# Order of the weight loads, a split first layer norm and a new priority table in an attention-plus-MLP kernel

## Chip, cores and metric

One core of a Trainium2 chip runs the whole kernel. The metric is device time in microseconds of one execution; the runs of a kernel are given by their median. The kernel before took 231.26 us (median of four: 230.19, 231.26, 231.27, 232.62).

## What is computed

One layer norm without weights feeds two branches, whose sum goes onto the input. Cut to what matters (S = 2048 rows, D = 512, 32 heads of 16, four segments of 512 rows, F = 1792; bf16):

```
xn = layernorm(x)                                   # (x - mean) / sqrt(var + 1e-5)
q, k, v = xn @ wq, xn @ wk, xn @ wv                 # split into 4 segments of 512 rows
for s in range(4):                                  # per head
    a_dot = softmax(q_s k_s^T / 4 + causal mask) v_s
    a_mem = phi(q_s) M / (phi(q_s) z + 1e-6)        # phi(t) = t + 1 where t > 0, else exp(t)
    o_s = g * a_mem + (1 - g) * a_dot               # g = sigmoid(beta), per head
    M += phi(k_s)^T v_s ;  z += sum(phi(k_s))
out = x + concat(o) @ wo + silu(xn @ w1) @ w2
```

## The kernel before

**Work and tiles.** Rows come in 16 tiles of 128, four per segment. TensorE makes, per segment, four tiles each of k, q (heads in eights) and v, fourteen tiles h of the MLP, the scores, the products with v (PV), the memory M, and the row products with w_2 and w_o. A gemm tile is four matmuls of 128x512 into one PSUM bank; a row product with w_2 is fourteen, with w_o four. Four banks (`ps`) serve all of these, and one buffer of four banks (`psS`) serves the scores.

**The beat.** Scores go in 72 quads, S0 to S71. Quad n needs `psS` free, so it waits for the exp of quad n-1 (E: 128x2048 on ScalarE, L890). GpSimd then masks the exp's result (M, L906, two instructions). Unit u is an eighth of the heads of a segment (16 units); PV u needs the masks of all quads with pieces of u, and two free banks. Between two scores TensorE has time for other matmuls, and the schedule fills it. VectorE empties the banks (kT, qT, V, hT "glu", EO, acc, o_t), ScalarE makes tanh for the MLP and the exp of phi, GpSimd the masked copies kB of k, the min of phi and small steps.

**Layer norm** (`ln`, L613). VectorE runs bn_stats and bn_aggr per tile (L621, L622; "stats"), GpSimd adds eps and raises to -0.5 (L629, L632; "rstd") for the groups of tiles in `LNG`, VectorE applies it (L640; "xn"). For segment 0, TensorE transposes xn and ScalarE (tiles 0 to 2) or VectorE (tile 3) copies it to xnT (L666, L668). For the other segments a DMA transpose from SP's queue does it (L674). phi(k) is transposed likewise into phiK (L781) for M.

**Memory and norm chains.** The softmax denominators go through DRAM and back in rows (L1101 to L1140, "Z": dZ, Zg, then a reciprocal on VectorE, a scaling Zr on GpSimd, dR, R), and so do the memory's (L1048 to L1077, "den"). VectorE then scales N with R (L1148, "a_t") and adds the memory's product psN (L1163, "oT").

**What sets the order.** Nothing is issued as it is written. Each step is a task with an engine, a guessed duration, dependences, the buffers that it takes, and a due time; `Sched.run` (L183) plays the tasks through and writes them out in the order that it finds: per engine the ready task with the least due time, scores and exps first. `Dn(n)` is a time, 12.5 + 2.3 n. `SHIFT` is a table by engine, label and count that shifts due times. The real waits (semaphores) are put in afterwards, from the buffers that instructions share; each DMA also waits for the landing of the eighth DMA before it. Each engine, and the DMA queue of SP, runs its list in that order without overtaking.

**Loads.** At the start (L456 to L478): x tiles 0 and 2 on SP's queue, 1 and 3 on ScalarE's; half of w_k on SP, half of w_q on ScalarE's, w_v on SP, the second half of w_q on ScalarE's, then on SP the first half of w_1 (896 KB), the second half of w_k, x tiles 4 to 7, the second half of w_1, beta. Later (`late_loads`, L1323): w_2 in two halves of 896 KB, w_o, and x of segments 2 and 3. There the planner may not start a load before a set time:

```
def at(k, n):
    k.ready = Dn(n)
    return k
for i, n in ((0, 6), (1, 9)):
    ld_2.append(at(load_w(w_2[:, c[i], :], kv(B_w2)[:, c[i], :], "SP", Dn(n), 5.5), n))
```

That time is the planner's alone. It settles the place in SP's order and makes no wait in the program.

Of the kernel before, what the change touches and what calls it, by code (L numbers as in the profile page):

```python
# [9 lines left out]
ALU = mybir.AluOpType  # L10
# [33 lines left out]
W2STEP = 2  # L44
NACC = 4
LOWB = 1
X3 = 37
LNG = ((0,), (1,), (2, 3))
XD = -1
SETUP = 9.0  # L50
HD = (12, 12)
LAST = 1
# [11 lines left out]
SEM = 0.05  # L64
SHIFT = {
    "DVE": {
        ("stats", 4): -4.9, ("stats", 5): -3.2, ("stats", 15): -0.9, ("xn", 13): -3.4,
        ("o_t", 12): 4.3,
    },
    "PE": {  # L70
        ("q1", 0): -9.5, ("q2", 0): -8.4, ("h0.0", 0): 21.4, ("h0.2", 0): 1.6, ("h0.4", 0): -10.5,
        ("h0.10", 0): 6.9, ("q4", 0): 7.2, ("k5", 0): -49.8, ("q5", 0): -4.6, ("k6", 0): 2.2,
        ("k7", 0): 15.9, ("q7", 0): 0.3, ("v10", 0): 14.1, ("v11", 0): -1.8, ("v12", 0): 18.7,
        ("v13", 0): -8.1, ("M0", 0): -9.3, ("w2.1", 0): -4.6, ("w2.3", 0): -1.8,
        ("wo.2", 0): 19.9, ("PV4", 0): 7.9, ("PV7", 0): 11.3, ("h1.0", 0): -69.3,
        ("h1.4", 0): -11.9, ("h1.6", 0): 41.7, ("h1.7", 0): 16.8, ("h1.10", 0): 13.8,
        ("h1.11", 0): -3.8, ("h1.12", 0): 16.4, ("h1.13", 0): -5.8, ("q8", 0): -2.2,
        ("k10", 0): -21.9, ("v22", 0): -9, ("M1", 0): 4.1, ("psN", 0): -21.9, ("w2.7", 0): 3.1,
        ("wo.4", 0): 13.2, ("wo.6", 0): 58.8, ("wo.7", 0): -7.6, ("PV8", 0): 9.2,
        ("PV10", 0): 8.6, ("h2.2", 0): 6.4, ("h2.3", 0): 11.6, ("h2.4", 0): 30.7,  # L80
        ("h2.5", 0): 7.1, ("h2.7", 0): -15.7, ("h2.8", 0): 5.8, ("h2.9", 0): -10.7,
        ("k13", 0): -12.4, ("v33", 0): 39.2, ("w2.8", 0): 4.3, ("w2.9", 0): -2.5,
        ("w2.10", 0): -50.3, ("w2.11", 0): 5.8, ("wo.9", 0): 5, ("wo.11", 0): 6,
        ("h3.3", 0): -14.2, ("h3.4", 0): -7.4, ("h3.8", 0): -15, ("h3.11", 0): -1.2,
        ("den3", 0): 52.5, ("outT3", 0): -2.2,
    },
    "ACT": {
        ("tanh", 6): -5.5, ("tanh", 18): -5.2,
    },
    "SP": {  # L90
        ("Z", 2): 30.5, ("Z", 10): 23.5, ("Z", 13): 18.6, ("Z", 23): -18.2, ("Z", 29): -3.1,
        ("den", 6): -3, ("den", 11): -9.4, ("den", 20): -36.7, ("mg", 4): 37.5,
    },
    "POOL": {
        ("phi", 13): -20.5, ("pq", 2): 3.8, ("kB", 22): 3.7, ("Zr", 2): 29, ("M58", 0): 50.8,
    },
}

# [222 lines left out]
def kernel(  # L321
# [25 lines left out]
    def sb(shape, dt, name):  # L347
        return cp.tile(shape, dt, name=name)
# [46 lines left out]
    rstd = sb([P, NT, 1], F32, "rstd")  # L395
    stt_t = [sb([P, nc.vector.BN_STATS_DIM], F32, f"st{i}") for i in range(4)]
    st_r = Ring(stt_t)
    lnc = sb([P, 2, 2], F32, "lnc")
    ident = sb([P, P], BF16, "ident")
    pm = sb([P, 2], F32, "pm")  # L400
# [46 lines left out]
    def load_w(dst, src, eng, due, vis, after=()):  # L447
        def fn():
            e = nc.sync if eng == "SP" else nc.scalar
            e.dma_start(out=dst, in_=src)  # L450
        return A(eng, 0.5, fn, due=due, vis=vis, seqdeps=after, label="w")
# [1 line left out]
    def kv(w):  # L453
        return w.rearrange("(ko ki) n -> ki ko n", ki=P)

    load_x(0, 1, "SP", 0, 2.85)  # L456
    load_x(1, 1, "ACTQ", 0, 2.95)
    load_x(2, 1, "SP", 0, 2.9)
    load_x(3, 1, "ACTQ", 0, 3.1)
    def halves(dst, src, n, which):  # L460
        c = slice(0, n) if which == 0 else slice(n, None)
        return dst[:, :, c], kv(src)[:, :, c]

    C2, F2 = D // 2, F // 2
    ld_o, ld_2 = [], []
    ld_k = [load_w(*halves(w_k, A_wk, C2, 0), "SP", 0, 5.2)]
    ld_q = [load_w(*halves(w_q, A_wq, C2, 0), "ACTQ", 0, 5.4)]
    ld_v = load_w(w_v[:], kv(A_wv), "SP", 0, 7.5)
    ld_q.append(load_w(*halves(w_q, A_wq, C2, 1), "ACTQ", 0, 7.0))
    ld_1 = [load_w(*halves(w_1, B_w1, F2, 0), "SP", 0.1, 9.5)]  # L470
    ld_k.append(load_w(*halves(w_k, A_wk, C2, 1), "SP", 0.15, 10.5))
    load_x(4, 2, "SP", 0.2, 11.5)
    load_x(6, 2, "SP", 0.2, 12.0)
    ld_1.append(load_w(*halves(w_1, B_w1, F2, 1), "SP", 0.3, 13.5))
    ld_b = load_w(
        bet[:], bass.AP(tensor=A_beta.tensor, offset=A_beta.offset, ap=[[0, P], [1, H]]),
        "SP", 0.35, 13.5,
# [1 line left out]
    def pool(dur, fn, deps=(), due=0.0, **k):  # L479
        return A("POOL", dur, fn, deps, due, **k)  # L480
# [130 lines left out]
                  mode="full", label="warm")  # L611

    def ln(s, due):  # L613
        for js in LNG if s == 0 else ((0, 1), (2, 3)):
            ag = []
            for j in js:
                t = s * TPS + j
                b = Buf(st_r)

                def f_st(t=t, b=b):  # L620
                    nc.vector.bn_stats(out=b.tile[:], in_=xt(t))  # L621
                    nc.vector.bn_aggr(out=mv[:, t, :], in_=b.tile[:])  # L622

                ag.append(A("DVE", 0.8, f_st, [xl[t]], due + 0.1 * j, takes=(b,), frees=(b,),
                            label="stats"))

            def f_r(t=s * TPS + js[0], n=len(js)):
                rs = rstd[:, t : t + n, :]
                nc.gpsimd.tensor_tensor(  # L629
                    out=rs, in0=mv[:, t : t + n, 1:2], in1=lnc[:, 0:n, 0:1], op=ALU.add  # L630
                )
                nc.gpsimd.tensor_tensor(out=rs, in0=rs, in1=lnc[:, 0:n, 1:2], op=ALU.pow)  # L632

            r = pool(1.0, f_r, ag + [c_ln], due + 0.1 * js[0], label="rstd")
            for j in js:
                t = s * TPS + j
                xb = Buf(xn_r)

                def f_x(t=t, xb=xb):
                    nc.vector.tensor_scalar(  # L640
                        out=xb.tile[:], in0=xt(t), scalar1=mv[:, t, 0:1],
                        scalar2=rstd[:, t, 0:1], op0=ALU.subtract, op1=ALU.mult,
                    )

                n = A("DVE", 0.35 if s == 0 else 0.48, f_x, [r], due + (XD if s == 0 else 0.1 * j),
                      takes=(xb,), frees=(xb,), label="xn")
                if s == 0:
                    pb = Buf(banks)

                    def f_t(xb=xb, pb=pb):  # L650
                        pv_ = pb.tile[:].bitcast(BF16)
                        for dt in range(DT):
                            nc.tensor.transpose(
                                pv_[:, dt * P : (dt + 1) * P], xb.tile[:, dt * P : (dt + 1) * P],
                                ident[:],
                            )

                    tr = A("PE", 0.26, f_t, [n, c_id], due, takes=(pb,), frees=(pb, xb), mode="full",
                           label="tr")
                    eng = "DVE" if j == 3 else "ACT"  # L660

                    def f_e(j=j, pb=pb, eng=eng):
                        o = xnT_b[0].tile[:, :, j * P : (j + 1) * P]
                        i = pb.tile[:].bitcast(BF16)[:, 0:D].rearrange("p (a b) -> p a b", a=DT)
                        if eng == "ACT":
                            nc.scalar.copy(out=o, in_=i)  # L666
                        else:
                            nc.vector.tensor_copy(out=o, in_=i)  # L668

                    e = A(eng, 0.5 if eng == "ACT" else 0.35, f_e, [tr], due,  # L670
                          takes=(xnT_b[0],), frees=(pb, xnT_b[0]), label="xnT")
                else:
                    def f_d(s=s, j=j, xb=xb):
                        nc.sync.dma_start(  # L674
                            out=xnT_b[s].tile[:, :, j * P : (j + 1) * P], in_=xb.tile[:],
                            transpose=True,
                        )
                    e = A("SP", 1.25, f_d, [n], due, vis=3.6, takes=(xnT_b[s],),
                          frees=(xb, xnT_b[s]), label="xnT")
                xnT_done[s].append(e)  # L680
# [186 lines left out]
    def quad(u, q):  # L867
# [21 lines left out]
        def f_x():  # L889
# [2 lines left out]
        e = A("ACT", 1.755, f_x, [sct], dn, vis=1.876 + 0.08, takes=(pb,), frees=(sbuf, pb),  # L892
              kind="exp", label=f"E{n}")
        last_exp[0] = e

        def f_m():
            for r in range(2):
# [343 lines left out]
    def tail():  # L1241
# [64 lines left out]
        for j in range(TPS):  # L1306
# [13 lines left out]
                nc.sync.dma_start(out=out_flat[t * P : (t + 1) * P, :], in_=ob.tile[:])  # L1320
            A("SP", 0.35, f_d, [e], 0, vis=1.75, frees=(ob,), label="out")

    def late_loads():  # L1323
        def at(k, n):
            k.ready = Dn(n)
            return k

        c = slice(0, FT // 2), slice(FT // 2, FT)
        for i, n in ((0, 6), (1, 9)):
            ld_2.append(at(load_w(w_2[:, c[i], :], kv(B_w2)[:, c[i], :], "SP", Dn(n), 5.5), n))  # L1330
        ld_o.append(at(load_w(w_o[:], kv(A_wo), "SP", Dn(12), 4.5), 12))
        load_x(8, 4, "SP", Dn(14), 4.5)
        load_x(12, 4, "SP", Dn(X3), 8.0, [xl[8]])
        at(xl[8], 14)
        at(xl[12], X3)

    ln(0, -4)
    for s in range(NSEG):
# [76 lines left out]
```

## Time and profile before

| | |
|---|---|
| median of four runs | 231.26 us |
| the profiled execution | 231.27 us |
| its span, first to last instruction | 229.5 us |
| TensorE clock granted | 0.998 |
| TensorE busy | 218.1 us (95%) |
| ScalarE, VectorE, GpSimd busy | 178.6, 173.4, 164.9 us |
| first score, last output step | 11.98 us, 225.75 us |
| DMA | 21.11 MB, mean 92 GB/s |

Times are microseconds from the first instruction. PE is TensorE's matmuls, PEld its weight loads, DVE VectorE, ACT ScalarE, POOL GpSimd, SP the engine that issues most DMAs; "SPq" marks an issue. L571 is the helper that records every matmul, so matmuls are told apart by their tiles. A line of waits reads: engine and line, what it waited for, total, times, longest. A line of the chain of waits: start, duration, what ran or was waited for. A line of the timeline: start, duration, engine, line, operation, tiles, count. Matmul ends are modelled: a 128x512 matmul is shown with 380 ns, though the next one starts 216 ns after it.

### The profile page before, as it was taken

What the parts mean: (1) busy time and instruction counts of PE and PEld (TensorE: products, weight loads), DVE (VectorE), ACT (ScalarE), POOL (GpSimd) and SP (SyncE); (2) the same over time, 40 slices, a digit from 0 to 9 for tenths busy, and PEclk for the clock granted to TensorE, in tenths of its full rate; (3) what the DMA queues carried; (4) which work ended last, traced back from release to release, by engine and by line L of the source; (5) the groups of instructions that cost most, each with busy time, mean ns of one, the idle gap of its engine ahead of it and who ended that gap; (6) DMA issues with size and microseconds to landing.
All of it is one profiled execution on the core that took longest, in us unless ns stands there. A gap on an engine that the chain in (4) does not pass through costs nothing.

```text
span 229.5 us, 6765 instructions
## 1 busy us (share of the span) xinstructions
PE 218.1 (95%) x2792; PEld 101.9 (44%) x2792; DVE 173.4 (76%) x302; ACT 178.6 (78%) x161; POOL 164.9 (72%) x285
## 2 busy tenths in 40 slices
PE   7799968999999999999999998999999999999993
PEld 7644433445444444434543444444454444445441
DVE  3689976698974789988894867988664798475972
ACT  2388995999898899896998796988898889895000
POOL 5749993897949659999999869689698465446500
PEclk9999999999999999999999999999999999999999
DMA  6975397341235221043256531010442200114202
GB/s 174 351 256 120 68 178 196 111 118 26 46 74 131 49 71 49 0 146 119 69 122 84 101 59 54 0 60 17 134 114 54 94 4 24 49 37 121 92 14 93
DMA packets 30708, 21.11 MB, mean 92 GB/s; under 512 B 15956, under 2 KB 29780, under 8 KB 30676
## 3 DMA queue, kind: packets, MB, share of 16 engines
q1 hardware_dynamic: 29332, 19.88, 33.7%
q10 hardware_dynamic: 1344, 0.79, 1.1%
q8 instruction: 22, 0.36, 0.7%
q14 instruction: 10, 0.08, 0.1%
HBM read 11.73 MB, written 2.64 MB: 63 GB/s over the span
## 4 chain that ended last, share of the span: by engine, by line
PE 71%; DMA 9%; DVE 9%; POOL 7%; issue 1%; SPq 1%; ACT 0%; POOLq 0%
PE ps L571 60%; PE psS L571 11%; POOL Pt L906 4%; DMA w_v<-in_A_wv_dram 4%; DMA xnT<-xn 3%; POOL kB L767 2%; DMA R<-dR 1%; DVE hT L1182 1%; DMA dR<-Zr 1%; DVE xn L640 1%; DVE V L827 1%; DVE st L621 1%; DVE kT L762 1%; DVE qT L810 1%; POOL pq L698 1%
## 5 line engine op out<-in xcount | busy, mean ns | idle before, releaser
L890 ACT ACTIVATE Pt<-psS 128x2048 bf16<-128x2048 f32 x72 | 135.6, 1883 | 20.3 <-PE psS L571 17.0
L906 POOL TENSOR_SCALAR_AFFINE_SELECT Pt<-Pt 64x512 bf16<-64x512 bf16 (+1 forms) x144 | 92.2, 641 | 34.9 <-ACT Pt L890 28.9
L571 PE MATMUL ps<-xnT,w 128*128 128x512 bf16 x224 | 57.4, 380 | 3.1 <-DMA xnT<-xn 3.1
L571 PE MATMUL ps<-w,hT 128*128 128x512 bf16 x196 | 48.7, 380 | 0.0
L1182 DVE SCALAR_TENSOR_TENSOR hT<-hT,ps 128x512 bf16<-128x512 bf16 x56 | 37.0, 678 | 10.2 <-ACT hT L1178 10.1
L1178 ACT ACTIVATE hT<-ps 128x512 bf16<-128x512 f32 x56 | 32.3, 605 | 2.8 <-PE ps L571 2.7
L571 PEld LDWEIGHTS <-w 128*128 128x128 bf16 x224 | 20.1, 98 | 26.8 <-issue 5.8
L571 PEld LDWEIGHTS <-hT 128*128 128x128 bf16 x224 | 20.3, 98 | 24.9 <-issue 2.6
L571 PE MATMUL psS<-qT,kB 32*128 32x256 bf16 (+5 forms) x640 | 28.7, 262 | 0.0
L767 POOL TENSOR_SCALAR kB<-kT,pm 128x512 bf16<-128x512 bf16 x30 | 22.6, 762 | 5.9 <-DVE kT L762 4.6
L571 PEld LDWEIGHTS <-kB 32*128 32x128 bf16 x640 | 11.6, 92 | 27.3 <-issue 25.9
L571 PE MATMUL ps<-Pt,VS 64*32 64x256 bf16 (+5 forms) x640 | 18.7, 261 | 1.6 <-DVE hT L1182 1.0
L571 PE MATMUL ps<-Pt,V 64*32 64x64 bf16 (+5 forms) x640 | 20.1, 260 | 0.0
L571 PE MATMUL ps<-xnT,w_q 128*128 128x512 bf16 (+1 forms) x76 | 18.3, 346 | 0.3 <-DMA w_q<-in_A_wq_dram 0.3
L571 PE MATMUL ps<-w_v,xnT 128*128 128x512 bf16 x64 | 17.7, 380 | 0.7 <-DMA w_v<-in_A_wv_dram 0.7
L571 PE MATMUL ps<-xnT,w_k 128*128 128x512 bf16 (+1 forms) x76 | 17.7, 346 | 0.0
L571 PEld LDWEIGHTS <-V 64*32 64x32 bf16 x640 | 14.0, 91 | 7.6 <-DVE hT L1182 2.5
L1207 DVE SCALAR_TENSOR_TENSOR acc<-ps,x_all 128x512 f32<-128x512 f32 x12 | 8.2, 681 | 8.9 <-PE ps L571 8.9
L962 DVE CAST N<-ps 128x512 bf16<-128x512 f32 x15 | 10.2, 682 | 5.7 <-PE ps L571 5.5
L571 PE MATMUL ps<-w_o,N 128*128 128x512 bf16 x54 | 14.3, 380 | 0.2 <-DVE V L827 0.2
L1084 POOL TENSOR_TENSOR pq<-pq,Dr 128x512 bf16<-128x512 bf16 x12 | 13.7, 1156 | 1.0 <-DMA Dr<-dE 0.6
L571 PEld LDWEIGHTS <-VS 64*32 64x32 bf16 x640 | 12.7, 91 | 2.4 <-DVE hT L1182 1.3
(96 smaller groups left out, 255.0 us busy)
## 6 DMA issues: line engine op xcount, KB each, us to landing
w<-in_B_w_dram SPq DMA_DIRECT2D x4, 896.0 KB
VS<-V SPq DMA_DIRECT2D x8, 264.0 KB
out_dram<-o_t SPq DMA_DIRECT2D x16, 128.0 KB
R<-dR SPq DMA_DIRECT2D x15, 128.0 KB
Dr<-dE SPq DMA_DIRECT2D x12, 128.0 KB
x_all<-in_A_x_dram SPq DMA_DIRECT2D x2, 512.0 KB
N<-O SPq DMA_DIRECT2D x12, 64.0 KB
w_k<-in_A_wk_dram SPq DMA_DIRECT2D x2, 256.0 KB
```

The costliest lines, as they stand in the source:

```text
L571: nc.tensor.matmul(o, lhsT=l, rhs=r, start=start, stop=stop, **k)
L621: nc.vector.bn_stats(out=b.tile[:], in_=xt(t))
L640: nc.vector.tensor_scalar(out=xb.tile[:], in0=xt(t), scalar1=mv[:, t, 0:1], scalar2=rstd[:, t, 0:1], op0=ALU.subtract, op1=ALU.mult,)
L698: nc.gpsimd.tensor_scalar(out=dst_b.tile[:], in0=dst_b.tile[:], scalar1=1.0, scalar2=0.0, op0=ALU.min, op1=ALU.max,)
L767: nc.gpsimd.tensor_scalar(out=kB[u].tile[:, :, KB * r : KB * r + KB], in0=kT[u].tile[:].rearrange("p (a b) -> p a b", b=KB), scalar1=pm[:, ...
L890: nc.scalar.activation(out=pb.tile[:], in_=psS[:], func=AF.Exp, scale=SCALE)
L906: nc.gpsimd.affine_select(out=v, in_=v, compare_op=ALU.is_ge, fill=0.0, base=0, pattern=pat, channel_multiplier=-1,)
L962: nc.vector.tensor_copy(out=dst.tile[:, dt, :], in_=buf.tile[:])
L1084: nc.gpsimd.tensor_tensor(out=pb.tile[:], in0=pb.tile[:], in1=rb.tile[:], op=ALU.mult)
L1178: nc.scalar.activation(out=hb.tile[:], in_=b.tile[:], func=AF.Tanh, scale=0.5)
L1182: nc.vector.scalar_tensor_tensor(out=hb.tile[:], in0=hb.tile[:], scalar=1.0, in1=b.tile[:], op0=ALU.add, op1=ALU.mult)
L1207: nc.vector.scalar_tensor_tensor(out=ab.tile[:], in0=b.tile[:], scalar=0.5, in1=xt(t), op0=ALU.mult, op1=ALU.add,)
```

## The change

Three things.

1. *Late loads.* The set times go. Instead `hold` gives a load's task a dependence on another task: w_2's first half on the four xnT transposes of segment 1, its second half on the exp of quad 9 (E9), w_o on E11, x of segment 2 on E13, x of segment 3 on E31. These are dependences among the planner's tasks.
2. *The start.* The second halves of w_q and w_k move behind the second half of w_1, all on SP; x tiles 4 to 7 move ahead of it. In segment 0 each row tile has its own rstd; eps is added on VectorE, behind bn_aggr, and GpSimd only raises to -0.5. Tile 2's mean and variance come from two ScalarE passes (Copy and Square, each with an accumulated sum), and two small VectorE operations bring them to the form that the rest expects. Tile 3's statistics may start no earlier than 6.4 us by the planner.
3. *The table.* `SHIFT` is another one, for VectorE, TensorE, GpSimd, ScalarE and SP, so the order changes on every engine, from the first layer norm to the last segment.

```diff
-X3 = 37
-LNG = ((0,), (1,), (2, 3))
+HOLD = {9: 1, 11: 2, 13: 3, 31: 4}
+LNG = ((0,), (1,), (2,), (3,))
+STJ = 3
+STR = 6.4
+ACTJ = 2
...
-    load_x(0, 1, "SP", 0, 2.85)
+    load_x(0, 1, "SP", 0, 3.4)
...
     ld_v = load_w(w_v[:], kv(A_wv), "SP", 0, 7.5)
-    ld_q.append(load_w(*halves(w_q, A_wq, C2, 1), "ACTQ", 0, 7.0))
     ld_1 = [load_w(*halves(w_1, B_w1, F2, 0), "SP", 0.1, 9.5)]
-    ld_k.append(load_w(*halves(w_k, A_wk, C2, 1), "SP", 0.15, 10.5))
-    load_x(4, 2, "SP", 0.2, 11.5)
-    load_x(6, 2, "SP", 0.2, 12.0)
-    ld_1.append(load_w(*halves(w_1, B_w1, F2, 1), "SP", 0.3, 13.5))
+    load_x(4, 2, "SP", 0.2, 9.8)
+    load_x(6, 2, "SP", 0.2, 10.0)
+    ld_1.append(load_w(*halves(w_1, B_w1, F2, 1), "SP", 0.3, 12.0))
+    ld_k.append(load_w(*halves(w_k, A_wk, C2, 1), "SP", 0.3, 12.5))
+    ld_q.append(load_w(*halves(w_q, A_wq, C2, 1), "SP", 0.3, 12.5))
...
+                if first and j == ACTJ:
+                    rt = float(D) ** -0.5
...
+                        nc.scalar.activation(
+                            out=scr[:], in_=xt(t), func=AF.Copy, scale=-rt / D, accum_out=nbias[:],
+                        )
...
+                        nc.scalar.activation(
+                            out=scr[:], in_=xt(t), func=AF.Square, scale=rt, bias=nbias[:],
+                            accum_out=vj,
+                        )
...
+                        nc.vector.tensor_scalar(
+                            out=vj, in0=vj, scalar1=EPS, scalar2=None, op0=ALU.add
+                        )
+                        nc.vector.tensor_scalar(
+                            out=mv[:, t, 0:1], in0=nbias[:], scalar1=-1.0 / rt, scalar2=None,
+                            op0=ALU.mult,
+                        )
...
+        if n in HOLD:
+            hold(late[HOLD[n]], [e])
...
+    def hold(t, deps):
+        for d in deps:
+            d.outs.append((t, True))
+            t.nwait += 1
...
+        for i in range(2):
+            ld_2.append(load_w(w_2[:, c[i], :], kv(B_w2)[:, c[i], :], "SP", Dn(6 + 3 * i), 6.5))
+        ld_o.append(load_w(w_o[:], kv(A_wo), "SP", Dn(12), 5.5))
         load_x(8, 4, "SP", Dn(14), 4.5)
-        load_x(12, 4, "SP", Dn(X3), 8.0, [xl[8]])
+        load_x(12, 4, "SP", Dn(37), 5.5)
+        late.extend([ld_2[0], ld_2[1], ld_o[0], xl[8], xl[12]])
+        hold(late[0], xnT_done[1])
```

## The prediction

> **What bounds the kernel.** I read the busy table first, then TensorE's waits, then the chain that ended last, then the stretch around the longest wait.
>
> ```profile
> PE 218.1 (95%) x2792; PEld 101.9 (44%) x2792; DVE 173.4 (76%) x302; ACT 178.6 (78%) x161; POOL 164.9 (72%) x285
> ```
>
> TensorE is the bound, but busy time alone can't say how tightly. The chain of waits can: from one score burst (psS) to the next it reads like this nearly everywhere:
>
> ```profile
> 61.21 0.33 PE psS L571 x12
> 61.54 2.26 PE ps L571 x10
> ```
>
> Ten 128x512 matmuls start 0.216 us apart, and the score with its two changes of tile shape costs 0.43, so a score period is 10 x 0.216 + 0.43 = 2.59 us. I took the start of all 72 scores from the trace and held each period against its own content. Priced so, the work from the first score (11.98 us) to the last matmul is 206.5 us; it took 213.9. A new order saves no TensorE work, only this difference. TensorE's waits:
>
> ```profile
> PE ps L571 <- DMA xnT<-xn: 3.1, 1, 3.1
> PE ps L571 <- DVE hT L1182: 1.0, 1, 1.0
> PE ps L571 <- DMA w_v<-in_A_wv_dram: 0.7, 1, 0.7
> PE ps L571 <- DVE N L1163: 0.7, 1, 0.7
> ```
>
> Against the period sum the same places cost more: the eighth period takes 6.29 us where 12 matmuls and a score need 3.02 (3.27 lost), the 33rd 3.99 for 2.66 (1.33), the 47th 3.57 for 2.45 (1.12). The other 1.7 us are scattered. The chain names what lay behind each:
>
> ```profile
> 2.19 8.09 DMA w_v<-in_A_wv_dram
> ...
> 28.72 6.68 DMA xnT<-xn
> ...
> 101.36 0.62 POOL pq L698
> 102.01 1.11 DVE pq L704
> 103.12 0.61 DVE hT L1182
> ...
> 131.78 3.02 DMA dR<-Zr
> 134.86 0.66 SPq L1140
> 135.57 3.36 DMA R<-dR
> 138.95 0.73 DVE N L1148
> ```
>
> See four different causes: a first weight that lands late; a transpose of 6.68 us; VectorE standing in order behind a GpSimd step; VectorE standing behind a round trip through DRAM. The transpose is the odd one. The DMA queue's own timeline:
>
> ```profile
> 20.27 2.61 SPq L674 DMA_TRANSPOSE xnT<-xn  x2
> 25.51 1.19 SPq L781 DMA_TRANSPOSE phiK<-pkT  x1
> 26.75 0.58 SPq L450 DMA_DIRECT2D w<-in_B_w_dram  x1
> 27.43 2.60 SPq L674 DMA_TRANSPOSE xnT<-xn  x2
> 30.36 5.61 SPq L781 DMA_TRANSPOSE phiK<-pkT  x2
> ```
>
> By the semaphores in the trace the transposes issued at 20.27 and 21.68 landed at 22.79 and 24.09, and the one at 25.51 at 27.80: 2.3 to 2.5 us each. Those at 27.43 and 28.72, behind the 896 KB load of w_2, landed at 34.92 and 35.40; w_2 itself at 34.26. Without it the last would have landed near 28.72 + 2.45 = 31.2, before TensorE wanted it (32.3).
>
> **The change, part by part.** *The holds.* They add dependences to the planner's tasks. The program built from them carries no wait for an exp on SP: each load there waits only for the DMA eight before it. What is real is the order on SP. Now all four xnT transposes and the second phiK go ahead of w_2's first half; third phiK, second half, fourth phiK, w_o and x8 follow. To price it, place the fourth xn on VectorE. It is busy without a gap from 13.16 to 28.46 in the trace, 24 operations up to and with that xn; now they are 26, with one more glu (0.65) and the four gcol operations (0.32), and it starts some 0.4 earlier: end at 28.46 - 0.4 + 0.97 = 29.0. Two transposes back to back (1.25 to issue, 2.45 to land) put the last xnT at 31.5 to 32. TensorE first wants it (q4) after the ninth score: 69 matmuls and one PV up to the eighth score where before there were 67, then nine: the eighth score at 30.64 - 0.63 (see the start) + 0.43, q4 at 30.44 + 0.43 + 9 x 0.216 + 0.43 = 33.2. Margin 1.3 us. Of what is queued behind on SP, the third phiK now lands behind w_2 (up to 7.5 us by the row above, near 40); its pkT buffer is next written after the 13th exp, near 46. The fourth phiK, behind w_2's second half, lands near 44, and M0 wants it near 47. **Gain 3.27**, bounds 0 (they collide anyway) and 3.27.
>
> [...]
>
> *The start.* The second half of w_q leaves the early queue (256 KB) and goes to the end, with k's. At the 313 to 391 GB/s that the windows from 5 to 15 us show that is 0.7 us less ahead of w_v, whose last part landed at 10.28; I take 9.6. Row statistics: the x tile's bn_stats and bn_aggr take 0.80 pitch on VectorE; tile 2's leave it for two passes on ScalarE, priced by the 128x512 copy there (0.59), so 1.2, in the idle time between the table load's end (4.12, now about 0.6 earlier, a w_q issue less ahead) and the first xnT copy (6.82). Bounds 0.9 and 3.8 (two exps of 128x2048). The added eps and var operations cost about 0.1 each (gcol: 0.32 for four), five of them. GpSimd's add (0.19, with its gap 0.27) falls out of every rstd. Sum: first xn at 5.40 instead of 5.79, last xn ends 8.45 instead of 8.93. But ahead of the fourth xnT copy VectorE now has a kB, which waits for ScalarE's kB, and a qT: copy ends near 10.35 (before 9.91). Then q0's last piece 10.4, its cast 10.8 to 11.2, first score 11.35 against 11.98; 0.63 earlier, less one matmul (0.22) that moved behind it. **Gain 0.4**, bounds -0.8 (if ScalarE's passes hold the copies 1.2) and 0.9.
>
> [...]
>
> *The table.* Same matmuls, one more behind the first score: 206.7 us. So it acts by cover alone. I counted for each PV how long after the last mask it needs TensorE comes to it. Before, eight of sixteen had under 0.5 us, PV6 among them, where TensorE lost 1.33; now six have: PV6 has 1.8 and PV5 2.0, and PV1, 8, 10, 12, 14 and 15 have 0.3 to 0.5, in stretches where GpSimd's masks run 0.07 to 0.9 late by the old rows. The first psN moves from the 46th to the 49th score. Its chain (GpSimd's Zr, then 7.2 us by the rows above to R) starts about one period later, so R lands 1.4 us before VectorE's a_t stands ready, but psN comes within 0.2 us of a_t. Both losses (2.45) may go; something else will be late. I book about half, as no row shows the new neighbours: **gain 1.25**, bounds -0.6 and 3.0.
>
> Sum on the profiled execution's span: 229.5 - 3.27 - 0.4 - 1.25 = 224.6. That run took 231.27, 1.77 more than its span and the median of the runs to 0.01: **226.3 us**.
>
> **The rivals.**
> *The other stalls keep their size, elsewhere.* For it: the planner guesses durations, and its first table left 4 us of late work behind. Then 229.5 - 3.27 - 0.4 + 1.77 = 227.6.
> *The holds do nothing.* No wait stands in the program; should phiK's wait for VectorE end early, or xn come late, w_2 meets the transposes again: 226.3 + 3.27 = 229.6. Against it: the phiK issued at 25.51, just ahead of w_2, was not disturbed.
> *GpSimd becomes the bound, and it is slower.* Between masks 25 and 36 GpSimd has 30.1 us of work (kB 0.69, phi 0.61, masks 0.9 and 1.37, pq 1.13, two rstd, Mbf, Zr) for 29.0 us of TensorE; before 28.6 for 28.7, and there masks already ran 1.83 us late. If every kB, phi and mask took its slowest row (1.23, 0.92, 1.71): 8 x 0.54 + 8 x 0.31 + 9 x 0.34 = 9.9 more, lag 11, less PV7's slack of 1.9: 9.1 lost. Against the 4.8 of transposes, start and 47th period: 235.6. It decides from a lag of 6.7. Against it: most rows sit at the median.
>
> **How the numbers follow.** Forecast 0.60 (224.2 to 227.5 alone), stalls elsewhere 0.21, holds idle 0.13, GpSimd 0.06. Low end 224.2: transposes, start 0.9 and all 3.0 of the later losses gone. High end 229.6: holds idle. Outside lie GpSimd and small tails. A measurement of this kernel tells about 1% from no change: faster means under 228.95. That holds the forecast and nearly all of the second case: 0.78; within 1%: 0.16; slower: 0.06.
>
> **What would show it.** Right: no TensorE wait for xnT; xnT landing 2.3 to 2.5 us after issue; the third phiK slow instead; w_v landing before 9.8; first score before 11.6; periods 33 and 47 without their loss. Wrong: a wait for xnT near 33; ScalarE's statistics ending after 6; masks over 2 us late near the 35th score; a new wait on VectorE of a microsecond or more, most likely before PV8, PV10 or psN.

## The result, and the profile after

The kernel after takes 232.93 us (median of 53 runs, 229.59 to 239.05); the kernel before 231.58 (79 runs, 229.89 to 234.38), and the forecast was 226.3, 6.6 us less. The ratio of the two kernels is 1.0014, 95% interval 0.9995 to 1.0032: by it, no difference that can be measured. It is taken over the fast runs alone, those within 1.5% of a kernel's fastest, which leaves out 23 of the 53 runs after; the medians of all runs stand 0.6% apart, and the section on the clock comes back to this. The profiled execution after took 231.89 us, span 230.1 (before 229.5), granted clock 0.998.

Busy table and TensorE's waits of the kernel after:

```profile
PE 218.7 (95%) x2792; PEld 102.1 (44%) x2792; DVE 171.8 (75%) x305; ACT 180.0 (78%) x165; POOL 164.4 (71%) x283
```

```profile
PE ps L577 <- DVE O L1009: 2.4, 2, 1.8
PE ps L577 <- DVE hT L1229: 1.7, 1, 1.7
PE psS L577 <- POOL ident masks.py:199: 1.4, 1, 1.4
PE ps L577 <- DVE qT L846: 0.8, 1, 0.8
PE ps L577 <- POOL Pt L953: 0.7, 1, 0.7
PE ps L577 <- DVE pq L749: 0.4, 1, 0.4
```

The busy table says nothing, as before. In the waits, the 3.1 us for xnT and the 0.7 for w_v are gone, and two VectorE lines stand in their place. (The line with `ident` is the wait ahead of the first matmuls, 1.4 us; both kernels have it.) SP's timeline after shows why xnT is no longer late:

```profile
21.98 9.57 SPq L719 DMA_TRANSPOSE xnT<-xn  x4
31.65 1.22 SPq L826 DMA_TRANSPOSE phiK<-pkT  x1
32.92 0.58 SPq L456 DMA_DIRECT2D w<-in_B_w_dram  x1
33.60 1.20 SPq L826 DMA_TRANSPOSE phiK<-pkT  x1
```

The four transposes, issued at 21.98, 23.28, 28.84 and 30.34, land 2.4 to 2.5 us later, the last at 32.84. The phiK transpose issued at 33.60, just behind w_2's half, is the slow one now: it lands at 40.10.

Priced as in the prediction (0.216 us per matmul, 0.43 per score), the 71 score periods lost 7.12 us before and 8.18 after:

| period (n-th score after the first) | lost before, us | lost after, us |
|---|---|---|
| 8 | 3.27 | 0.26 |
| 27 | below 0.1 | 0.61 |
| 31 | below 0.1 | 1.83 |
| 33 / 34 | 1.33 / below 0.1 | below 0.1 / 0.45 |
| 44 | below 0.1 | 2.00 |
| 47 | 1.12 | 0.36 |
| 65 and 67 | below 0.1 each | 0.89 and 0.80 |

So 3.01 us were won at the eighth period, and 4.1 lost elsewhere, net. The last score starts 1.15 us later (207.41 for 206.26): first score 0.34 earlier, losses 1.06 more, and two matmuls (0.43) that moved between the two; behind the last score some 0.5 is saved. Where the new losses begin stands in VectorE's timeline:

```profile
81.83 0.69 DVE L1009 CAST O<-ps 128x512 bf16<-128x512 f32 x1 [1.41 <-DMA N<-O]
...
83.64 0.94 DVE L1168 RECIPROCAL Zf<-Zg 128x128 f32<-128x128 bf16 x1
...
91.83 1.52 DVE L1195 TENSOR_TENSOR N<-N,R 128x512 bf16<-128x512 bf16 x2
93.52 0.62 DVE L1195 TENSOR_TENSOR N<-N,R 128x512 bf16<-128x512 bf16 x1 [0.17 <-DMA R<-dR]
94.06 1.64 DVE L749 SCALAR_TENSOR_TENSOR pkT<-kT,pkT 128x512 bf16<-128x512 bf16 x1
95.63 0.08 DVE L749 DVE_READ_ACCUMULATOR pkT<-kT,pkT 128x1 f32 x1
95.63 0.68 DVE L1229 SCALAR_TENSOR_TENSOR hT<-hT,ps 128x512 bf16<-128x512 bf16 x1
...
131.87 0.69 DVE L1009 CAST O<-ps 128x512 bf16<-128x512 f32 x1 [2.78 <-DMA N<-O]
```

The bracket is idle time and what ended it. There is one buffer O. It is free for the next unit only when four small DMAs have copied its rows into N (N<-O, "mg"). VectorE stands 1.41 and 2.78 us for them (periods 27 and 44). Period 31 is VectorE's order: three products with R and a pkT step stand ahead of the hT at 95.63 that TensorE waits for. The third product starts as its R lands (93.49; idle 0.17 us), the first two take 0.73 and 0.86 us where most others take 0.41 to 0.43, and the pkT step takes 1.64 where others take 0.66 to 1.15; what stretches these is not shown. SP's queue shows why N<-O is late (here `x4` and `x2` count issues, and the time is that of issuing them):

```profile
76.12 1.21 SPq L826 DMA_TRANSPOSE phiK<-pkT  x1
77.42 2.52 SPq L1163 DMA_DIRECT2D N<-O  x4
...
123.52 3.14 SPq L826 DMA_TRANSPOSE phiK<-pkT  x2
126.75 2.49 SPq L1163 DMA_DIRECT2D N<-O  x4
```

The new table puts phiK transposes, and in the first segment the den chain (dD, Dg), ahead of them. They land at 81.71 and 131.65. Before, they were issued from 70.92, landed at 76.07, and O was wanted at 81.80.

### The profile page after: what moved, and what is told of

The parts are those of the page before. It is cut to its first block, busy times and chain, and to the rows that moved or that the text cites. A ratio compares the mean times of both kernels' runs of the same rounds, so it can differ in the third digit from the quotient of the medians.

```text
span 230.1 us, 6774 instructions
## 1 busy us (share of the span) xinstructions
PE 218.7 (95%) x2792; PEld 102.1 (44%) x2792; DVE 171.8 (75%) x305; ACT 180.0 (78%) x165; POOL 164.4 (71%) x283
## 4 chain that ended last, share of the span: by engine, by line
PE 67%; DVE 9%; DMA 8%; POOL 7%; SPq 3%; issue 3%; ACT 2%; DVEq 0%; POOLq 0%; ACTq 0%
PE ps L577 54%; PE psS L577 13%; POOL Pt L953 3%; DMA N<-O 2%; POOL pq L1131 2%; SPq L1163 2%; DMA R<-dR 2%; DMA Dr<-dE 2%; DVE kT L807 1%; DVE hT L1229 1%; DVE pkT L749 1%; DMA dR<-Zr 1%; DVE N L1009 1%; SPq L826 1%; DVE O L1009 1%
## 5 line engine op out<-in xcount | busy, mean ns | idle before, releaser
L577 PE MATMUL ps<-w,hT 128*128 128x512 bf16 x196 | 47.5, 380 | 0.0
L812 POOL TENSOR_SCALAR kB<-kT,pm 128x512 bf16<-128x512 bf16 x30 | 20.6, 696 | 6.4 <-DVE kT L807 5.1
L577 PE MATMUL ps<-Pt,V 64*32 64x256 bf16 (+5 forms) x640 | 19.8, 260 | 0.7 <-POOL Pt L953 0.7
L577 PE MATMUL ps<-w_v,xnT 128*128 128x512 bf16 x64 | 16.6, 380 | 1.1 <-DVE qT L846 0.8
L577 PE MATMUL ps<-xnT,w_q 128*128 128x512 bf16 (+1 forms) x76 | 17.5, 346 | 0.0
L1009 DVE CAST O<-ps 128x512 bf16<-128x512 f32 x15 | 10.2, 682 | 4.2 <-DMA N<-O 4.2
```

What stands on the lines that cost most here:

```text
L577: nc.tensor.matmul(o, lhsT=l, rhs=r, start=start, stop=stop, **k)
L812: nc.gpsimd.tensor_scalar(out=kB[u].tile[:, :, KB * r : KB * r + KB], in0=kT[u].tile[:].rearrange("p (a b) -> p a b", b=KB), scalar1=pm[:, ...
L1009: nc.vector.tensor_copy(out=dst.tile[:, dt, :], in_=buf.tile[:])
```

## The experiments

The theory: the table's order on SP makes N<-O late, and VectorE and GpSimd, which run in order, pass that on. The rival: VectorE and GpSimd are simply full there, and any wait removed comes back elsewhere. In the diffs, `nth(engine, label, n)` is the n-th task of that label in the planner's finished order, and `move(a, b)` puts task a directly behind b; everything else keeps its place. Medians stand beside the ratio to the kernel before, run on the same chip.

**b_w2: the load alone.** On the kernel before.

```diff
+    move(nth("SP", "w", 6), nth("SP", "phiK", 1))    # w_2's first half
```

> The kernel before, with nothing changed but the place of the first half of w_2 on SP: behind the second phiK, and so behind all four xnT transposes. If the transposes behind that load are what the eighth period lost, the xnT wait of 3.1 us goes, the last two land 2.3 to 4 us after their issue, and the time falls by 2.5 to 3.3 us, ratio about 0.987. Rival: the planned work behind it is late already, and TensorE meets the next wait 3 us sooner: a gain under 1 us, ratio above 0.996.

228.65 us, ratio 0.9876 (0.9832 to 0.9919); the median fell by 2.94. The last two xnT, issued at 26.59 and 28.09, landed at 30.66 and 31.20. TensorE's waits:

```profile
PE ps L571 <- DVE hT L1182: 1.7, 2, 0.9
PE psS L571 <- POOL ident masks.py:199: 1.4, 1, 1.4
PE ps L571 <- DVE N L1163: 0.8, 1, 0.8
PE ps L571 <- ACT xnT L666: 0.2, 1, 0.2
```

No wait for xnT, and what was behind it kept its size within 0.3 us, but for a new 0.93 at the ninth period. One moved load gives what the whole change was to give in its first part. Not all of the 2.94 is the wait, though. In the profile, the lost time of all periods fell by 2.2 us (3.27 less, 0.93 new), and the runs before on this chip that had a granted clock of 0.996 or more have a median of 230.24 (10 runs). Beside them the gain is 1.6 us; the rest goes with the lower clock of the other 13 runs before.

**a_w2early: the load back in front, in the kernel after.**

```diff
+    move(nth("SP", "w", 7), nth("SP", "xnT", 2), before=True)
```

> The kernel after, with the first half of w_2 put back ahead of the third xnT transpose on SP. If its place makes the wait, the last two xnT land 6 to 7.5 us after their issue, TensorE waits some 2 to 3.5 us for them near 33, and the kernel is 1 to 1.5% slower than the one before (ratio 1.010 to 1.016). Rival (the new places of the xn on VectorE decide): no wait for xnT, ratio 1.000 to 1.003.

233.37 us, ratio 1.0059 (1.0021 to 1.0098), and no wait for xnT. The rival holds:

```profile
25.03 0.58 SPq L456 DMA_DIRECT2D w<-in_B_w_dram  x1
29.32 3.13 SPq L719 DMA_TRANSPOSE xnT<-xn  x2
```

Here the load is issued 4.3 us ahead of the first transpose and has landed by 30.40; the transposes, issued at 29.32 and 31.23, land at 32.31 and 33.71, 3.0 and 2.5 us later. In the kernel before, the load went 0.7 us ahead, landed at 34.26, and they took 7.5 and 6.7. What cost here was not to stand behind a big load (3.0 us at 4.3 us behind it), but to stand close behind it (7.5 at 0.7); with the new table the hold on w_2 was not needed.

**a_mg: N<-O as early as their data allow.**

```diff
+    for g in range(4):
+        move(nth("SP", "mg", 3), nth("SP", "Z", 1))
+    for g in range(4):
+        move(nth("SP", "mg", 7), nth("SP", "Z", 9))
```

> The kernel after, with the four transfers N<-O of the first and of the second segment moved on SP from behind the phiK transposes to directly behind the dZ reads. Theory 1 (late merges: the single O buffer is held by them, VectorE stands, and with it Zf and the chain to psN): VectorE no longer waits for N<-O before its evacuations at 81.8 and 131.9, the lost time of score periods 27 (0.61 us), 44 (2.00) and most of 31 (1.83) goes, 3.5 to 4.4 us in all, ratio to before about 0.983. Theory 2 (VectorE and GpSimd are full there, and another wait takes the place): less than 1 us gained, ratio 0.997 to 1.003. The transposes moved behind may land up to 2.5 us later; both theories allow that at no cost, a wait of TensorE for phiK would be a third answer.

239.16 us, ratio 1.0315 (1.0247 to 1.0384): 6 us worse than the kernel after, an answer that neither theory has, and near the third: not TensorE, but VectorE and ScalarE wait for what was moved behind:

```profile
80.66 0.95 DVE L1105 RECIPROCAL Dg<-Dg 128x128 f32<-128x128 f32 x1 [4.31 <-DMA Dg<-dD]
```

```profile
133.40 0.63 ACT L740 ACTIVATE pkT<-kT 128x512 bf16<-128x512 bf16 x1 [4.92 <-DMA phiK<-pkT]
133.93 1.86 ACT L935 ACTIVATE Pt<-psS 128x2048 bf16<-128x2048 f32 x1
```

The merges wait at the head of SP's queue for dZ to land, and what they were moved past waits with them: Dg, for which VectorE stands 4.31 us, then phiK, whose pkT buffer ScalarE wants; behind ScalarE's wait stands the exp at 133.93. TensorE lost 2.95 and 4.38 us in one piece. None of these DMAs had the slack that I gave them.

**a_mg2: N<-O as early as nothing else is late for it.**

```diff
+    for g in range(4):
+        move(nth("SP", "mg", 3), nth("SP", "den", 1))
+    for g in range(4):
+        move(nth("SP", "mg", 7), nth("SP", "phiK", 9))
```

> The kernel after, with the four N<-O of each of the first two segments brought forward only as far as nothing else on SP is late for it: in the first segment behind Dg<-dD and ahead of one phiK transpose, in the second between two phiK transposes. They issue 1.3 and 1.8 us earlier. Theory 1 (SP's order is a trade between these DMAs, and the merges were the ones left behind): VectorE's waits for N<-O shrink from 1.4 and 2.8 us to under 0.3 and about 1, no new wait on phiK or Dg of over 0.5 us, periods 27 and 44 lose 1.5 to 2.2 us less in all; the profiled span 227.7 to 228.6 against 230.1. Theory 2 (any move on this queue only shifts the wait to the transposes): span 229.5 or more.

232.5 us, ratio 1.0000 (0.9965 to 1.0036), span 230.7: a miss. Period 27 lost nothing, so its loss was N<-O's landing; 44 lost 1.66 instead of 2.00, and period 34 went from 0.45 to 1.55. Read alone, this speaks for the rival.

**a_o2: two O buffers, order unchanged.** The planner still counts one, so the order stays.

```diff
-    O_b = [Buf(O_r) for _ in range(NSEG)]
+    O_t = [sb([P, DT, L], BF16, f"O{i}") for i in range(2)]
+    O_b = [OBuf(O_r, O_t[s % 2]) for s in range(NSEG)]    # .tile is O_t[s % 2]
```

> The kernel after, in the same order, with two O buffers in turn instead of one, so that VectorE's evacuation need not wait for N<-O however late that lands. Theory 1 (the O buffer is what VectorE stands for): as for the moved transfers, 3 to 4.4 us gained, ratio about 0.984, though N<-O still lands at 81.7 and 131.7. If the late landing itself costs (N is late for the norm), part of it stays and the gain is 1 to 2.5 us. Theory 2 (VectorE and GpSimd are full): less than 1 us.

231.68 us, ratio 0.9990 (0.9950 to 1.0031), span 228.1. Periods 27 and 44 lose nothing (2.61 us back), 31 keeps 1.26, and 34 rises to 1.54. Half for the theory: the O buffer was what VectorE stood for; but part of the gain came back as a wait 7 periods on.

**a_o2mg2, a_o2zg: is R late for N<-O's sake?** Both earlier edits together; then Zg ahead of N<-O as well.

```diff
+    move(nth("SP", "Z", 2), nth("SP", "mg", 0), before=True)
```

> Two O buffers and the earlier N<-O together. If the losses of periods 27 and 44 come from the O buffer and the one of period 31 from the late R (dZ to R starts late because VectorE reached Zf late), both go: periods 27, 31 and 44 lose under 1 us in all (4.4 after), span about 227. If R is late for another reason (the order of Zg on SP, GpSimd's Zr), period 31 keeps 1.2 us or more as with two O buffers alone, span about 228.

> Two O buffers and the earlier N<-O as in the run before, and in the first segment Zg<-dZ issued ahead of the four N<-O instead of behind them and a phiK transpose: 4 us earlier (76 instead of 80.0). If period 31 (1.82 us lost there) is VectorE standing in order at the first R, and R is late because Zg was issued late, VectorE no longer waits 1.5 us for Zg, R lands 1.4 us earlier or more, and period 31 loses 0.6 us or less: span 227.4 to 227.9 against 228.8. Rival (R is late because of GpSimd's Zr or the four steps through DRAM themselves): period 31 keeps over 1.2 us.

230.49 us, 0.9946 (0.9910 to 0.9982), and 230.95 us, 0.9959 (0.9923 to 0.9996). Period 31 kept its loss in both (1.82 and 3.33, the second in a profile with a granted clock of 0.990, see below), though Zf ran 0.6 us earlier in the second. Zg was not what held R: in that trace GpSimd's Zr is done at 84.77, and on SP dR stands behind three Dr loads of the den chain (84.15 to 86.12, dR at 86.21). That these hold R is read from the rows; no run moves them. Both misses.

**a_at, a_o2at: VectorE's order.** Two of the products with R go behind the hT, kT and qT that TensorE waits for.

```diff
+    for i in range(2):
+        move(nth("DVE", "a_t", 1), nth("DVE", "glu", 23), before=True)
```

> The kernel after, with nothing changed but two of VectorE's four products N x R of the first segment, which stand waiting for R at 92 to 93.5: they go four instructions later, behind the hT, kT and qT that TensorE waits for. If VectorE's order there is what period 31 loses (1.83 us), it loses 0.4 or less, TensorE's gap of 1.66 us at 94.7 is gone, span about 228.6 against 230.1, and the median falls by 1.5 us or more (232.9 to about 231.2). Rival (VectorE has no room there: the work behind is late too): the gap moves to the next w_o rows or PV, span 229.5 or more.

> The same with two O buffers: the losses of periods 27, 31 and 44 (4.4 us in the kernel after) should all be under 0.4 each. Period 34 (1.54 with two O buffers) and 64 to 67 (1.65) belong to GpSimd and stay. Span about 227, no TensorE gap over 1.3 us, so no halved clock behind one: runs between 228.5 and 230, median about 229, where two O buffers alone had 231.7. Rival: the gap at 94 is back in half of the runs and the median stays above 230.5.

a_at: 232.54 us, 1.0015 (0.9978 to 1.0053). Period 31 lost nothing (1.83 in the kernel after), but 34 lost 2.01 instead of 0.45, and 44 lost 3.88 instead of 2.00, with the clock at 0.5 behind its gap of 2.24 us. a_o2at: 230.91 us, 0.9962 (0.9927 to 0.9997); 27 and 44 nothing, 31 0.61, 34 3.19, again with the clock at 0.5, for 3.4 us behind a gap of 1.67 us. So the loss of period 31 was VectorE's order, but the time did not fall as forecast: the loss moved on to the next place, as the rival says.

**a_o2pq, a_o2atpq: GpSimd's order in the third segment.** In the kernel after, one multiply with Dr (pq) stood waiting for its DMA, with the masks of two quads behind it:

```profile
185.93 1.16 POOL L1131 TENSOR_TENSOR pq<-pq,Dr 128x512 bf16<-128x512 bf16 x1 [2.14 <-DMA Dr<-dE]
187.04 2.58 POOL L953 TENSOR_SCALAR_AFFINE_SELECT Pt<-Pt 64x512 bf16<-64x512 bf16 x4
```

```diff
+    move(nth("POOL", "pq", 7), nth("POOL", "phi", 22))
```

> Two O buffers, and GpSimd's fourth pq multiply of the third segment, which stands in order waiting for its Dr from DRAM, moved behind the next four masks and the phi step behind them. If that wait is what the periods from 64 to 67 lose (0.69, 0.16 and 0.80 us with two O buffers alone), the masks 62 and 63 are no longer 2 to 3 us late and these periods lose under 0.5 us together: span 1.0 to 1.4 us below that of two O buffers alone (228.1). Rival: the moved multiply delays VectorE's pq and the third den as before, and period 67 keeps its 0.8.

> The same, and GpSimd's fourth pq multiply of the third segment behind the masks and phi step that it held, which took the losses of periods 64 to 67 from 1.65 to 0.41: span about 226, median 227.7 to 228.3, close to the forecast made before the change was run. Rival: as above.

a_o2pq: 231.17 us, 0.9938 (0.9897 to 0.9979); periods 64 to 67 lose 0.41 together. The span (229.1) missed its forecast: at period 31 TensorE stood 2.35 us in one piece, and the clock was 0.5 for 3.4 us from 97.96 on; periods 31 and 32 lost 4.2 together. a_o2atpq: 229.25 us, 0.9911 (0.9875 to 0.9947), span 227.2; it lost 4.66 us in all, 2.03 of it at period 34, and period 67 kept 0.85. The median is 1 us above what was expected.

**a_final: order or a full GpSimd at period 34?** On top of a_o2atpq. VectorE waited 1.30 us at 100.4 for a phi step that stood on GpSimd behind a multiply, and GpSimd had waited 1.4 us for Dr before:

```profile
88.51 1.15 POOL L1142 TENSOR_TENSOR pq<-pq,Dr 128x512 bf16<-128x512 bf16 x1 [1.41 <-DMA Dr<-dE]
...
101.67 1.11 DVE L760 SCALAR_TENSOR_TENSOR pq<-qT,pq 128x512 bf16<-128x512 bf16 x1 [1.30 <-POOL pq L754]
```

```diff
+    move(nth("POOL", "kB", 16), nth("DVE", "kT", 10))
+    move(nth("POOL", "kB", 17), nth("POOL", "kB", 16))
+    move(nth("POOL", "pq", 0), nth("POOL", "kB", 17))
+    move(nth("POOL", "phi", 13), nth("POOL", "pq", 3), before=True)
```

> The kernel of the run before (two O buffers, two VectorE products later, one GpSimd multiply of the third segment later), and in the first segment on GpSimd the two kB steps ahead of the pq multiply that stands 1.4 us waiting for Dr, and the phi step that VectorE waits 1.3 us for at 100.4 ahead of the fourth pq multiply. If period 34 (2.03 us lost, TensorE gap of 1.66 us) is the place of these steps, it loses 0.7 or less and no gap over 1 us is left: span about 225.7, no run at a clock under 0.997, median 227.3 to 227.8. If GpSimd is simply full there (its masks run 2.3 to 3.6 us late from period 27 to 34), the wait moves to a mask ahead of the next PV: 1.5 us or more stays, median 228.5 or more.

227.66 us (227.18 to 229.97), ratio 0.9843 (0.9791 to 0.9894), span 225.5. Period 34 loses 0.35, 32 still 0.87, all periods together 3.07. The masks still run 1.8 to 3.0 us late from period 27 to 35, and it hardly matters: GpSimd was not full, four steps stood in the wrong places (which of them counted most was not taken apart). TensorE's three longest waits:

```profile
PE psS L588 <- POOL ident masks.py:199: 1.4, 1, 1.4
PE ps L588 <- DVE qT L857: 0.8, 1, 0.8
PE ps L588 <- DVE hT L1240: 0.7, 1, 0.7
```

With this the rival falls, as the reason that the waits came back. They did come back, one after the other, but each time at one step or a few out of place. It took a second O buffer and seven moved steps, all on VectorE and GpSimd, to come within 1.4 us of the forecast. SP's order stayed as the table has it: moves on SP alone (a_mg, a_mg2) gained nothing.

**b_w2q, b_best: the start, and the old table.** b_w2, and w_q's second half on SP behind w_1's second half; then the phi step that VectorE waited for at period 33 ahead of one mask.

```diff
+    move(nth("ACTQ", "w", 1), nth("SP", "w", 4))              # issued on SP
+    move(nth("POOL", "phi", 14), nth("POOL", "M30", 0), before=True)    # b_best alone
```

> The kernel before with the w_2 half moved behind the transposes as in the run before it, and the second half of w_q moved from ACT's queue to SP, behind the second half of w_1, as the change has it; row statistics stay on VectorE. If the early queue's bytes set the start, w_v lands near 9.0 instead of 9.7 to 10.3 and the first score starts 0.2 to 0.7 us earlier, time about 228.2, ratio 0.985. Rival: the first score hangs on the norm of the fourth tile, as in the kernel after, and starts no earlier: 228.6.

> The kernel before with the two moves on the load queues (w_2's first half behind the transposes, w_q's second half behind w_1's) and one on GpSimd: the phi step that VectorE's pq waits 1.1 us for at 98.4 goes ahead of one mask. If period 33 loses its 1.46 us to that order alone, it keeps 0.4 or less and the time is 226.7 to 227.0 (ratio 0.979); if the mask moved behind it then holds the next PV, the loss stays: 227.9.

b_w2q: 227.88 us, 0.9840 (0.9798 to 0.9882). w_v lands at 8.98 (9.70 in b_w2), and the first score starts at 11.68 (11.55): the rival holds on the first score, which gains nothing, though the time is nearer the first forecast. Of the 0.8 us that the median fell, 0.6 are seen at period 47 (0.61 lost for 1.25). b_best: 227.41 us, 0.9816 (0.9778 to 0.9855); period 33 loses 0.50 instead of 1.46. It is the fastest median here: three moved steps on the old table, without the change. b_w2q is also the nearest that a run comes to the change without its table: it has two of the change's load moves, w_2 behind the transposes and w_q to the end, and takes 227.88, where the forecast without the table's gain is 227.6 and the kernel after takes 232.93.

**a_best.** a_o2zg and a_o2pq together, and the first pq multiply behind the two kB steps.

```diff
+    move(nth("POOL", "pq", 0), nth("POOL", "kB", 17))
```

> The same, and on GpSimd the two multiplies that stand waiting for Dr from DRAM moved behind work that is ready: the first pq multiply behind the mask and the two kB steps that follow it, the fourth of the third segment behind the next masks and a phi step. If GpSimd's waits are what is left in periods 34 (1.55) and 64 to 67 (1.69 together), both fall below 0.5: span about 225.5, ratio 0.978. Rival: the multiplies are then late for psN and den, and the loss stays within 0.5 us of the run before.

233.81 us, 1.0086 (1.0047 to 1.0126). In this order the multiply came behind the fourth Dr load, which reuses its buffer. So it read the fourth tile's reciprocals in place of the first's, and GpSimd waited 4.69 us for that load. The run says nothing on GpSimd's waits; a_final makes the move rightly.

**b_again: the clock.** The kernel before once more.

> The kernel before once more, for one profile. Its times lie in two groups, near 230.2 at a granted clock of 0.998 to 1.000 and near 231.8 at 0.990 to 0.993. If the clock is halved for some 3.4 us behind the xnT wait of 3.1 us, as it is in other profiles here behind TensorE gaps of 2.35 us and more, a profile of the second group shows PEclk at 0.5 between 35 and 40 us and nowhere else; if the lower mean comes from elsewhere, PEclk dips at another place. A profile of the first group (about 4 in 10) tells nothing.

229.94 us at clock 0.999, a profile of the first group: inconclusive.

**What the clock does.** In other profiles the granted clock is seen to fall from 1.00 to 0.50 at a TensorE gap. The windows of a_o2zg (start and end, length, busy time of PE, PEld, DVE, ACT, POOL with counts, granted clock, DMA share, GB/s), around a TensorE gap of 2.44 us that ends at 97.27:

```profile
94.00:96.00 2.00, 0.83 (x4) 0.29 (x3) 1.61 (x3) 1.93 (x2) 1.88 (x2) 1.00 0.48 131
96.00:98.00 2.00, 0.73 (x3) 0.29 (x3) 2.00 (x5) 0.00 (x0) 1.85 (x4) 0.86 0.66 231
98.00:100.00 2.00, 2.00 (x12) 0.48 (x12) 1.68 (x4) 0.95 (x2) 1.93 (x3) 0.50 0.00 0
100.00:102.00 2.00, 1.78 (x8) 0.82 (x8) 0.37 (x1) 1.98 (x2) 1.92 (x3) 0.79 0.00 0
102.00:104.00 2.00, 2.00 (x13) 0.70 (x11) 1.32 (x3) 0.94 (x1) 1.83 (x4) 1.00 0.00 0
```

From 97.4 to 100.8 the clock is 0.5, so that gap cost an estimated 1.7 us (half of 3.4) more than itself. With the lower clock goes a part of the spread of one kernel's times, and of the 1 us by which the median after stands above its profiled run:

| | runs at clock 0.996 and above | median, us | runs below | median, us |
|---|---|---|---|---|
| before (115 runs beside the experiments, five chips) | 33 | 230.26 | 82 | 232.23 |
| after (54) | 27 | 231.54 | 27 | 233.95 |
| b_w2, b_w2q, b_best, a_final (24) | 24 | 227.4 to 228.6 | 0 | |

The four kernels of the last row have no TensorE gap over 1 us in their profiles behind the first score, and all of their runs have a clock of 0.997 or more. At equal clock the kernel after is 1.3 us behind the one before, close to what its lost time says (1.06); the ratio of 1.0014 hides it. The clock is not all of the spread: the 27 runs after in the first column reach from 229.59 to 233.98. That the lower clock of the kernel before sits behind its xnT gap is argued from these rows, not shown.

## Why the prediction was wrong

*Where the 6.6 us went.* The profiled span came out 5.5 us above its forecast (230.1 for 224.6). 5.3 of these are the table: 1.25 booked, 4.1 lost. All other terms make 0.2 together. The last 1.1 is the median's distance to its profiled run.

*The holds* ("Gain 3.27, bounds 0 and 3.27"): right in size on the trace. The eighth period lost 3.01 less, and the third phiK took 6.5 us as foretold. That b_w2 gained 2.94 in the median is in part luck: 0.93 came back at the ninth period, and the lower clock of most runs before, which I had not counted, added to the gain. The cause was too narrow: a_w2early shows that the load could go first: with the load 4.3 us ahead, the transpose landed 3.0 us after its issue.

*The start* ("Gain 0.4, bounds -0.8 and 0.9"): within the bounds. First score 11.64, less the matmul that moved: 0.12. w_v landed at 9.00 (I said 9.6), but TensorE then waited 0.8 for VectorE's qT, and the last xn ended at 8.94, not 8.45. The two ScalarE passes took 1.58 from start to end (0.63 and 0.72, each with 0.19 to read the sum), not 1.2, and tile 3's rstd took GpSimd 0.68. Profiles of kernels with the same start put the first score anywhere from 11.35 to 12.59, so 0.1 can't be told from nothing.

*The table* ("gain 1.25, bounds -0.6 and 3.0"): this step failed, by sign and size. The old 33rd and 47th losses went (2.1 us won), as booked. The new ones (27, 31, 44, 65, 67: 6.1 us) are three times those; the net loss of 4.1 is seven times the bound. That the table is the step that failed is shown from two sides: b_w2q, with the old table, comes to 227.88, and a_final, with the new one and its worst-placed steps moved, to 227.66. I had counted the slack of every PV against its masks, and of one R; I had not placed the other DMAs of SP, though the order showed four N<-O behind a phiK transpose, and one O buffer. My list of signs had "a new wait on VectorE of a microsecond or more, most likely before PV8, PV10 or psN": it came at the evacuations of the first units of the next segments and at the products with R.

*The rivals.* "The holds do nothing" fell. "The other stalls keep their size, elsewhere" (227.6) was nearest in kind, and too small: they more than doubled. "GpSimd becomes the bound" fell with a_final: its sign came true there, masks 1.8 to 2.5 us late near the 35th score, but its price did not: 0.35 us lost at period 34, and the masks stayed far from the lag of 6.7 us that it needed.

*The baseline.* I set the sum on one profiled execution and added 1.77. That run was at a clock of 0.998; about seven in ten runs of the kernel before (82 of 115) are below 0.996. Its 231.27 is 1 us above the median of the runs at 0.996 and above (230.26), and that it met the median of all runs is chance. In b_w2, where the long gap is gone, all six runs have a clock of 0.997 or more, and its times spread by 0.3 us. The kernel after has two new gaps, of 1.66 and 1.84 us. In its profile the clock stayed at 1.00 at both, but half of its runs (27 of 54) are below 0.996; that such a gap gives the lower clock back is my estimate, not shown. (A slip beside it: the low end of the range is 224.1 by its own terms, not 224.2.)

## What to carry to other kernels

Here one DMA queue and three engines each ran their lists in order (in a_mg VectorE stood 4.31 us for a load kept behind others), and such an order is only as good as its worst-placed step: for every DMA that changes places, set its landing against the moment of its reader, and look for single buffers that it frees. A wait removed shows the next one, so one experiment that gains nothing does not mean that the engines are full; go on until the waits no longer come back, or until an engine truly has no gap. A long gap on TensorE can cost more than its length (an estimated 1.7 us more at the one of 2.44 us in a_o2zg), and medians differ with the clock (the kernel before: 230.26 us at 0.996 and above, 232.23 below), so compare runs at equal clock too.

## What the runs showed of the hardware

- A transpose on SP's queue that was issued 0.7 to 2 us behind an 896 KB load landed 6.2 to 7.5 us after issue in all 16 cases of these traces; 2.6 to 3.6 us behind the load it took 4.2 to 5.5 us (5 cases), and 4.3 us behind it 3.0 (one case). With no load or copy of SP in flight at its issue it took 2.3 to 2.6 us in seven cases of ten (of 212), and up to 4.6 in the others, so a load ahead is not the only thing that slows it.
- The granted clock fell to 0.50 at TensorE gaps of 1.67, 2.24, 2.35, 2.44, 3.34 and 4.38 us, between 0.9 us before the gap's end and 1.4 us behind it, and stayed there for 3.4 us at five of them and 6.8 at the one of 3.34; at gaps of 1.66, 1.84, 2.66, 2.95 and 3.10 us elsewhere it stayed at 1.00. Length alone does not decide; what does is not shown.
- On the way through DRAM and back, dR took 1.4 to 3.7 us from issue to landing (median 2.6 over all traces) and R 2.6 to 4.6 (median 3.0).
